# One visit of a chunked recurrence behind each output unit of a fused retention and feed-forward kernel

## The chip, the cores and the metric

One core of one Trainium2 chip. The metric is device time in microseconds (us). Most executions of one kernel agree within about 1 us.

## The reference, cut to what matters

A retention layer (a linear recurrence with a decay per head), then a feed-forward with a leaky ReLU, all in float32:

```python
batch, n_heads, seq, head_dim = (4, 8, 768, 64)
for t in range(S):
    state = gamma * state + einsum('bhd,bhe->bhde', k[:, :, t], v[:, :, t])
    y[:, :, t] = scale * einsum('bhd,bhde->bhe', q[:, :, t], state)
x = y.transpose(0, 2, 1, 3).reshape(3072, 512)
h = x @ w_in                       # 512 -> 2048
return maximum(0.01 * h, h) @ w_out   # 2048 -> 512
```

## The kernel before

The sequence is cut into six parts of 128 tokens, all four batches in each; parts are numbered 0 to 5. For a part and a batch the recurrence is four groups of small matmuls: *scores* (keys against queries, tiles of 64x64), which VectorE masks; *reads* of the running state (64x64); *values* (masked scores against values, 128x64); and *state sums* (128x64). VectorE then *takes* the tokens into x and brings the state up to date. When a part is complete it makes three *differences* t of x.

The feed-forward multiplies in a scheme of seven products instead of eight, M1 to M7, in *hidden units* and *output units* (`seven`). The products share four banks, A to D, of PSUM, the memory that TensorE's products are written to: M1 and then M2 on top of it in A, M6 and M7 in B, M5 and M3 in C, M4 in D. M1 is needed alone, so ScalarE copies it out before M2 is added.

Before the change each part is computed while the part ahead of it is in the feed-forward. TensorE stops twice per two batches: once for their scores, three products later for reads, values and state sums, in banks of their own (two pairs, tag "att").

```python
    def two_banks(name):
        return psum.tile([128, 2, HP, C], FP32, tag="att", bufs=2, name=name)
    def score(c, b):
        x = heads[c, b][0]
        ps = scores[c, b] = two_banks(f"ap_{c}_{b}")
        for a in range(HP):
            for u in range(2):
                for j in range(2):
                    nc.tensor.matmul(ps[ts(u, 64), j, a, :], lhsT=x[ts(j, 64), 1, a, ts(u, 64)],
                                     rhs=x[ts(j, 64), 0, a, :])
    def masked(c, b):
        am = work.tile([128, 2, HP, C], FP32, tag="am", bufs=2, name=f"am_{c}_{b}")
        nc.vector.tensor_tensor(
            out=am.rearrange("p j a t -> p (j a) t"),
            in0=scores[c, b].rearrange("p j a t -> p (j a) t"),
            in1=mask.unsqueeze(1).to_broadcast([128, H, C]), op=ALU.mult)
        scores[c, b] = am
    ...
    def reads(c, b):
        x = heads[c, b][0]
        ps = sums_at[c, b] = two_banks(f"yp_{c}_{b}")
        for j, m, i, a in pairs:
            nc.tensor.matmul(ps[ts(i, 64), j, m, :], lhsT=st[b][ts(j, 64), a, :],
                             rhs=x[ts(j, 64), 0, a, :], start=(m == 0), stop=False,
                             skip_group_check=True)
    def values(c, b):
        if c == 0:
            sums_at[c, b] = two_banks(f"yp_{c}_{b}")
        y, am, ps = heads[c, b][1], scores.pop((c, b)), sums_at[c, b]
        for j, m, i, a in pairs:
            nc.tensor.matmul(ps[ts(i, 64), j, m, :], lhsT=y[:, 1, 2 * a + j, :],
                             rhs=am[:, j, a, :], start=(c == 0 and m == 0), stop=True,
                             skip_group_check=True)
    def state(c, b):
        y = heads.pop((c, b))[1]
        sp = for_state(sums_at[c, b])
        for a in range(HP) if c < NC - 1 else ():
            sums_of(sp, y, a)
    ...
    def tokens_taken(c, b, xb):
        ps = sums_at[c, b]
        th, o = divmod(b * C, N)
        blocks = xb.rearrange("p (kh th) k n -> p kh th k n", th=2)[:, :, th, :, ds(o, C)]
        nc.vector.tensor_tensor(out=blocks, in0=ps[:, :, 0 : HP // 2, :], in1=gq, op=ALU.mult)
    def state_taken(c, b):
        ps = sums_at.pop((c, b))
        if 0 < c < NC - 1:
            nc.vector.tensor_tensor(out=st[b], in0=st[b], in1=for_state(ps), op=ALU.add)
            nc.vector.tensor_tensor(out=st[b], in0=st[b],
                                    in1=gc.unsqueeze(2).to_broadcast([128, HP, D]), op=ALU.mult)
    def products(c, bs):
        for f in (reads, values, state):
            for b in bs:
                f(c, b)
    def stage_y(c, bs, xb):
        products(c, bs)
        for b in bs:
            taken(c, b, xb)
            n = c * B + b + AHEAD
            if c > 1 and n < NC * B:
                load(*divmod(n, B))
    ...
    def differences(x, t, last=True):
        minus(t[:, 0], x[:, 1], x[:, 0])
        minus(t[:, 1], x[:, 3], t[:, 0])
        minus(t[:, 2], x[:, 2], t[:, 1])
        if last:
            last_difference(x)
    ...
    def seven(tiles, name, takes, takes_half=None, order=ORDER):
        banks = {}
        which = [("M1", "A", 0, 0), ("M6", "B", 5, 5), ("M5", "C", 4, 4), ("M4", "D", 3, 6),
                 ("M2", "A", 2, 2), ("M7", "B", 1, 1), ("M3", "C", 6, 3)]
        for m, bank, sa, sb in (which[i] for i in order):
            first = bank not in banks
            split = takes_half is not None and bank == "C"
            if first and split:
                banks[bank] = [two_banks(f"{bank}{i}_{name}")[:, 0].rearrange("p a t -> p (a t)")[:, 0:N]
                               for i in range(2)]
            elif first:
                banks[bank] = psum.tile([128, 2, N], FP32, tag="ff", bufs=4, name=f"{bank}_{name}")
            ps = banks[bank]
            for i in range(2):
                half = ps[i] if split else ps[:, i, :]
                for n, (w, x, t) in enumerate(tiles):
                    rhs = x[:, sb] if sb < 4 else t[:, sb - 4]
                    for k in range(2):
                        nc.tensor.matmul(
                            half, lhsT=block(w, sa)[:, k, ts(i, 128)], rhs=rhs[:, k, :],
                            start=(first and (i == 0 or split) and n == 0 and k == 0),
                            stop=(n == len(tiles) - 1 and k == 1), skip_group_check=True)
                if split and m == "M3":
                    takes_half(i, half)
            if not (split and m == "M3"):
                takes(m, ps)
            yield
    ...
    def hidden(c, u, x, t, g, gd, order=ORDER):
        got = {}
        at = f"{c}_{u}"
        def leaky(i):
            nc.scalar.activation(g[:, i], g[:, i], AF.Prelu, alpha=0.01)
        def takes(m, ps):
            if m == "M1":
                got["m1"] = temp("m1", at)
                nc.scalar.copy(out=got["m1"], in_=ps)
            elif m == "M6":
                got["u2"] = temp("u2", at)
                plus(got["u2"], got["m1"], ps)
            elif m == "M5":
                got["m5"] = temp("m5", at)
                nc.scalar.copy(out=got["m5"], in_=ps)
            elif m == "M4":
                got["m4"] = ps
            elif m == "M2":
                nc.scalar.activation(g[:, 0], ps, AF.Prelu, alpha=0.01)
            elif m == "M7":
                u3 = got["m1"]
                plus(u3, u3, ps)
                plus(g[:, 3], u3, got["m5"])
                leaky(3)
                plus(g[:, 2], u3, got["m4"])
                leaky(2)
            elif m == "M3":
                plus(g[:, 1], got["u2"], ps)
                leaky(1)
                differences(g, gd)
        return seven([(2 * u, x, t)], f"h{at}", takes, order=order)
    ...
    for c in range(2, NC):
        more = c + 1 < NC
        os[c] = new_o(c)
        if more:
            xs[c + 1] = new_x(c + 1)
        for p in range(NU // 2):
            pair = []
            for u in (2 * p, 2 * p + 1):
                pair.append(new_g(c, u))
                at = {}
                if more and u == 2 * p:
                    at = {1: [scored(c + 1, u), scored(c + 1, u + 1)],
                          4: [read(c + 1, u, u + 1)]}
                run(hidden(c, u, *xs[c], *pair[-1][1:]), at)
            at = {1: [differ(c + 1)]} if p == 1 and more else {}
            run(output(c, os[c], pair, p == 0, p == NU // 2 - 1), at)
```

## Time and profile before

| | before |
|---|---|
| median of the first 3 runs, and of all 6 beside the changed kernel | 666.92 us, 666.81 us |
| span of the profiled run | 664.9 us |
| TensorE busy, VectorE, ScalarE | 99%, 56%, 26% |
| TensorE waiting for another engine | 2.2 us, all in the first 13 us |
| stops for the recurrence, parts 2 to 5 | 16 |

The page and the views are read in the prediction below. A row of a timeline reads: start in us, length from the first start to the last end, engine, line, operation, output<-input, shapes, count, and in brackets the idle time before it with what ended it. The lengths of neighbours overlap (in the prediction's lines, 403.20 + 1.89 is past the next start, 404.93), so the difference of two *starts* is what a stretch takes. The first figure of a matmul's shapes, 64\*64, 128\*64 or 128\*128, is the part of TensorE's array that it uses; I call it the *mode*, and 128\*128 *full size*.

I use one further number throughout. The start of an execution varies, so I take from the single records (every matmul's own start in the trace) the time from the start of the first product of the first output unit (58.1 us in) to the end of the last matmul, and call it the **long stretch**. Before: 603.61 us.

### The profile page before, as it was taken

What the parts mean: (1) busy time and instruction counts of PE and PEld (TensorE: products, weight loads), DVE (VectorE), ACT (ScalarE), POOL (GpSimd) and SP (SyncE); (2) the same over time, 40 slices, a digit from 0 to 9 for tenths busy, and PEclk for the clock granted to TensorE, in tenths of its full rate; (3) what the DMA queues carried; (4) which work ended last, traced back from release to release, by engine and by line L of the source; (5) the groups of instructions that cost most, each with busy time, mean ns of one, the idle gap of its engine ahead of it and who ended that gap; (6) DMA issues with size and microseconds to landing.
All of it is one profiled execution on the core that took longest, in us unless ns stands there. A gap on an engine that the chain in (4) does not pass through costs nothing.

```text
span 664.9 us, 10405 instructions
## 1 busy us (share of the span) xinstructions
PE 659.4 (99%) x4505; PEld 573.6 (86%) x4505; DVE 373.9 (56%) x570; ACT 175.8 (26%) x322; POOL 20.1 (3%) x22
## 2 busy tenths in 40 slices
PE   8999999999999999999999999999999999999998
PEld 5888888888888888888888888888888888888886
DVE  5789969889888676325543613663431444431342
ACT  5854555264261002212201311210221220221210
POOL 0000000000000111001000100100100000000000
PEclk9999999999999999999999999999999999999999
DMA  8920312313222453003012100301300001000001
GB/s 327 403 97 33 126 64 79 112 65 113 109 85 75 166 184 127 1 1 128 1 46 81 64 1 1 127 1 64 128 1 0 2 0 45 19 1 1 0 1 63
DMA packets 15758, 48.92 MB, mean 74 GB/s; under 512 B 1753, under 2 KB 2009, under 8 KB 15713
## 3 DMA queue, kind: packets, MB, share of 16 engines
q1 hardware_dynamic: 15696, 48.24, 20.1%
q8 instruction: 35, 0.57, 0.3%
q14 instruction: 11, 0.08, 0.0%
q10 hardware_dynamic: 16, 0.02, 0.0%
HBM read 41.97 MB, written 6.29 MB: 73 GB/s over the span
## 4 chain that ended last, share of the span: by engine, by line
PE 99%; DMA 1%; DVE 0%; issue 0%
PE B_o L414 13%; PE A_o L414 13%; PE C_o L414 12%; PE C_h L414 12%; PE B_h L414 12%; PE A_h L414 12%; PE D_o L414 6%; PE D_h L414 6%; PE ap L165 4%; PE yp L193 4%; PE d L436 2%; PE yp L184 2%; PE yp L208 1%; DMA qk<-in_qk_dram 1%; PE sums L208 0%; PE idle L626 0%
## 5 line engine op out<-in xcount | busy, mean ns | idle before, releaser
L414 PE MATMUL A_h<-x,w 128*128 128x256 f32 x368 | 87.0, 379 | 0.0
L414 PEld LDWEIGHTS A_h<-x,w 128*128 128x128 f32 x368 | 69.9, 190 | 9.6 <-issue 0.2
L414 PE MATMUL A_o<-g,w 128*128 128x256 f32 x288 | 68.0, 379 | 0.0
L449 ACT ACTIVATE g<-g 128x512 f32<-128x512 f32 x69 | 42.0, 630 | 92.4 <-DVE g L361 92.4
L414 PEld LDWEIGHTS A_o<-g,w 128*128 128x128 f32 x288 | 54.8, 190 | 7.4
L454 ACT COPY m<-A_h 128x512 f32<-128x512 f32 x23 | 13.4, 582 | 143.6 <-PE A_h L414 103.9
L361 DVE TENSOR_TENSOR m<-m,B_h 128x512 f32<-128x512 f32 x23 | 15.8, 686 | 55.5 <-PE B_h L414 55.5
L361 DVE TENSOR_TENSOR m<-m,B_o 128x512 f32<-128x512 f32 x16 | 11.0, 685 | 63.9 <-PE B_o L414 63.9
L238 DVE TENSOR_TENSOR x<-yp,dec 128x512 f32<-128x512 f32 x24 | 16.4, 689 | 49.7 <-PE yp L208 35.6
L414 PE MATMUL C_h<-t,w 128*128 128x256 f32 x184 | 44.1, 383 | 0.0
L414 PE MATMUL B_h<-x,w 128*128 128x256 f32 x184 | 44.1, 383 | 0.0
L414 PE MATMUL B_h<-t,w 128*128 128x256 f32 x184 | 43.5, 379 | 0.0
L414 PE MATMUL D_h<-t,w 128*128 128x256 f32 x184 | 43.5, 379 | 0.0
L414 PE MATMUL C_h<-x,w 128*128 128x256 f32 x184 | 43.5, 379 | 0.0
L414 PEld LDWEIGHTS C_h<-t,w 128*128 128x128 f32 x184 | 34.5, 190 | 5.5 <-issue 0.9
L414 PEld LDWEIGHTS B_h<-t,w 128*128 128x128 f32 x184 | 35.0, 190 | 4.7
L414 PEld LDWEIGHTS D_h<-t,w 128*128 128x128 f32 x184 | 35.0, 190 | 4.7
L414 PEld LDWEIGHTS C_h<-x,w 128*128 128x128 f32 x184 | 35.0, 190 | 4.7
L414 PEld LDWEIGHTS B_h<-x,w 128*128 128x128 f32 x184 | 34.5, 190 | 5.0 <-issue 0.3
L364 DVE TENSOR_TENSOR gd<-g,gd 128x512 f32<-128x512 f32 x48 | 37.1, 773 | 1.7
L170 DVE TENSOR_TENSOR am<-ap,mask 128x1024 f32<-128x1024 f32 x24 | 28.5, 1220 | 10.8 <-PE ap L165 10.8
L414 PE MATMUL B_o<-gd,w 128*128 128x256 f32 x144 | 34.0, 379 | 0.0
(118 smaller groups left out, 1019.0 us busy)
## 6 DMA issues: line engine op xcount, KB each, us to landing
raw<-in_weights_dram SPq DMA_DIRECT2D x31, 512.0 KB, 4.3
qk<-in_qk_dram SPq DMA_DIRECT2D x19, 512.0 KB, 3.8
kv<-in_kv_dram SPq DMA_DIRECT2D x17, 512.0 KB, 4.4
out_dram<-o SPq DMA_DIRECT2D x23, 256.0 KB, 2.1
in<-in_qk_dram SPq DMA_DIRECT2D x3, 512.0 KB, 8.7
in<-in_kv_dram SPq DMA_DIRECT2D x3, 512.0 KB, 8.5
kv<-in_kv_dram SPq DMA_DIRECT2D x4, 256.0 KB, 7.0
o_in<-in_qk_dram SPq DMA_DIRECT2D x2, 512.0 KB, 8.6
```

The source lines that it names most:

```text
L165: nc.tensor.matmul(ps[ts(u, 64), j, a, :], lhsT=x[ts(j, 64), 1, a, ts(u, 64)], rhs=x[ts(j, 64), 0, a, :])
L170: nc.vector.tensor_tensor(out=am.rearrange("p j a t -> p (j a) t"), in0=scores[c, b].rearrange("p j a t -> p (j a) t"), in1=mask.unsqueeze ...
L184: nc.tensor.matmul(ps[ts(i, 64), j, m, :], lhsT=st[b][ts(j, 64), a, :], rhs=x[ts(j, 64), 0, a, :], start=(m == 0), stop=False, skip_group_ ...
L193: nc.tensor.matmul(ps[ts(i, 64), j, m, :], lhsT=y[:, 1, 2 * a + j, :], rhs=am[:, j, a, :], start=(c == 0 and m == 0), stop=True, skip_grou ...
L208: nc.tensor.matmul(sp[ts(j, 64), a, :], lhsT=y[:, 0, 2 * a + j, :], rhs=y[:, 1, 2 * a + j, :], start=start, stop=True, skip_group_check=True)
L238: nc.vector.tensor_tensor(out=blocks, in0=ps[:, :, 0 : HP // 2, :], in1=gq, op=ALU.mult)
L361: nc.vector.tensor_tensor(out=out, in0=a, in1=b, op=ALU.add)
L364: nc.vector.tensor_tensor(out=out, in0=a, in1=b, op=ALU.subtract)
L414: nc.tensor.matmul(half, lhsT=block(w, sa)[:, k, ts(i, 128)], rhs=rhs[:, k, :], start=(first and (i == 0 or split) and n == 0 and k == 0), ...
L436: nc.tensor.matmul(banks[r][:, i, :], lhsT=block(2 * u, r + 2 * kh)[:, k, ts(i, 128)], rhs=x[:, 2 * kh + th, k, :], start=(step == 0 and i ...
L449: nc.scalar.activation(g[:, i], g[:, i], AF.Prelu, alpha=0.01)
L454: nc.scalar.copy(out=got["m1"], in_=ps)
```

## The change

Its intent: TensorE should leave its full-size products less often. The scores of the *next* two batches are computed within the visit for the sums of the present two, so that one visit behind each output unit takes the place of two stops. The scores go to the feed-forward's PSUM banks, which are idle between two units once the last sum has read its own. The hidden unit that follows a completed part has its products in the order M1, M2, M6, M5, M4, M7, M3 (`FIRST`), so that two products which need nothing new cover the making of t. A third buffer for masked scores, and loads of queries and keys one visit ahead, make room for it.

The diff, cut to its core; left out are buffer names and small helpers:

```diff
+    def new_am(c, b):
+        i = turn[0]
+        turn[0] = (i + 1) % (3 if (c, b) >= (2, 2) else 2)
+        if i < 2:
+            return work.tile([128, 2, HP, C], FP32, tag=f"am{i}", name=f"am_{c}_{b}")
+        place = new_t(1, f"am_{c}_{b}").rearrange("p i k n -> p (i k n)")[:, 0 : 2 * HP * C]
+        return place.rearrange("p (j a t) -> p j a t", j=2, a=HP)
 ...
-    def stage_y(c, bs, xb):
-        products(c, bs)
 ...
+    def ahead(c, b):
 ...
+            if b == 2:
+                room[c] = new_o(0).rearrange("p i k n -> p (i k n)")
 ...
+    def score_apart(c, b):
+        x = heads[c, b][0]
+        ps = scores[c, b] = [psum.tile([128, HP, C], FP32, tag="ff", bufs=4, name=f"ap{j}_{c}_{b}")
+                             for j in range(2)]
+        for a in range(HP):
+            for u in range(2):
+                for j in range(2):
+                    nc.tensor.matmul(ps[j][ts(u, 64), a, :], lhsT=x[ts(j, 64), 1, a, ts(u, 64)],
+                                     rhs=x[ts(j, 64), 0, a, :])
+
+    def masked_apart(c, b):
+        am = new_am(c, b)
+        for j, ps in enumerate(scores[c, b]):
+            nc.vector.tensor_tensor(out=am[:, j], in0=ps,
+                                    in1=mask.unsqueeze(1).to_broadcast([128, HP, C]), op=ALU.mult)
+        scores[c, b] = am
+
+    def visit(c, b, following=None, complete=False):
+        bs, xb = (b, b + 1), xs[c][0]
+        more = [(following[0], following[1] + i) for i in range(2)] if following else [None, None]
+        early, late = more
 ...
+        do(score_apart, early)
+        for i in bs:
+            reads(c, i)
+        do(masked_apart, early)
+        for i in bs:
+            values(c, i)
+        do(score_apart, late)
+        for i in bs:
+            state(c, i)
+        do(masked_apart, late)
+        for i in bs:
+            tokens_taken(c, i, xb)
+        if complete:
+            if xs[c][1] is None:
+                xs[c][1] = new_t(c, f"t_{c}")
+            differences(*xs[c])
+        for i in bs:
+            state_taken(c, i)
+        for i in bs:
+            if c + 1 < NC:
+                ahead(c + 1, i)
+        for at in more:
+            do(load_kv, at)
+        for at in more:
+            do(decay_v, at)
 ...
+    FIRST = (0, 4, 1, 2, 3, 5, 6)
 ...
-                at = {0: [scored(2, 2 * c), scored(2, 2 * c + 1)],
-                      3: [read(2, 2 * c, 2 * c + 1)]}
-                if c == 1:
-                    put(at, s4=[differ(2)])
+                if c == 0:
+                    at = {0: [scored(2, 0), scored(2, 1)], 3: [lambda: visit(2, 0)]}
+                else:
+                    at = {1: [lambda: ahead(2, 2), lambda: ahead(2, 3)],
+                          2: [lambda: load_kv(2, 2), lambda: load_kv(2, 3)],
+                          4: [scored(2, 2), scored(2, 3)]}
 ...
+    if NC > 2:
+        visit(2, 2, (3, 0) if NC > 3 else None, complete=True)
     for c in range(2, NC):
 ...
-                at = {}
-                if more and u == 2 * p:
-                    at = {1: [scored(c + 1, u), scored(c + 1, u + 1)],
-                          4: [read(c + 1, u, u + 1)]}
-                run(hidden(c, u, *xs[c], *pair[-1][1:]), at)
-            at = {1: [differ(c + 1)]} if p == 1 and more else {}
-            run(output(c, os[c], pair, p == 0, p == NU // 2 - 1), at)
+                run(hidden(c, u, *xs[c], *pair[-1][1:], order=ORDER if u else FIRST), {})
+            run(output(c, os[c], pair, p == 0, p == NU // 2 - 1), {})
+
+            if c + 1 < NC and p == 0:
+                xs[c + 1] = new_x(c + 1)
+                visit(c + 1, 0, (c + 1, 2))
+            elif c + 1 < NC and p == NU // 2 - 1:
+                visit(c + 1, 2, (c + 2, 0) if c + 2 < NC else None, complete=True)
```

More of the change, by code (lines that the diff above doesn't have):

```diff
@@ L166, in score, with new_t, new_o @@
                                      rhs=x[ts(j, 64), 0, a, :])
+    turn = [0]
+    def new_am(c, b):
[5 more added lines that the diff above has]
+        return place.rearrange("p (j a t) -> p j a t", j=2, a=HP)
+    def new_t(c, name):
+        return work.tile([128, 3, 2, N], FP32, tag=f"t{int(c == 1)}", name=name)
+    def new_o(c, name="o"):
+        return work.tile([128, 4, 2, N], FP32, tag=f"o{int(c > 0)}", name=f"{name}_{c}")
     def masked(c, b):
-        am = work.tile([128, 2, HP, C], FP32, tag="am", bufs=2, name=f"am_{c}_{b}")
+        am = new_am(c, b)
         nc.vector.tensor_tensor(
@@ L200, in state @@
     def state(c, b):
-        y = heads.pop((c, b))[1]
+        y = heads[c, b][1]
         sp = for_state(sums_at[c, b])
@@ L251, in products @@
                 f(c, b)
-    def stage_y(c, bs, xb):
-        products(c, bs)
-        for b in bs:
-            taken(c, b, xb)
-            n = c * B + b + AHEAD
-            if c > 1 and n < NC * B:
-                load(*divmod(n, B))
+    def ahead(c, b):
+        if c >= NC:
+            return
+        if b < 2:
+            x = work.tile([128, 2, HP, C], FP32, tag="qk", bufs=AHEAD, name=f"qk_{c}_{b}")
+        else:
+            if b == 2:
+                room[c] = new_o(0).rearrange("p i k n -> p (i k n)")
+            x = room[c][:, ds((b - 2) * 2 * HP * C, 2 * HP * C)]
+            x = x.rearrange("p (s a t) -> p s a t", s=2, a=HP)
+        heads[c, b] = [x, None]
+        load_qk(c, b)
@@ new lines, in load_kv @@
+    def load_kv(c, b):
+        y = work.tile([128, 2, H, D], FP32, tag="kv", bufs=AHEAD, name=f"kv_{c}_{b}")
+        heads[c, b][1] = y
+        nc.sync.dma_start(out=y, in_=kv[c, b])
+    room = {}
+    def score_apart(c, b):
[7 more added lines that the diff above has]
+                                     rhs=x[ts(j, 64), 0, a, :])
@@ new lines, in masked_apart, with do @@
+    def masked_apart(c, b):
+        am = new_am(c, b)
+        for j, ps in enumerate(scores[c, b]):
[6 more added lines that the diff above has]
+        early, late = more
+        def do(f, at):
+            if at is not None:
+                f(*at)
+        do(score_apart, early)
[23 more added lines that the diff above has]
+            do(decay_v, at)
@@ L540, in new_x @@
         x = tile_x(c)
-        t = work.tile([128, 3, 2, N], FP32, tag="t", bufs=2, name=f"t_{c}")
-        return x, t
-    def new_o(c):
-        return work.tile([128, 4, 2, N], FP32, tag="o", bufs=2, name=f"o_{c}")
+        return [x, new_t(c, f"t_{c}") if c < 3 else None]
     slot = [0]
@@ L567, in scored @@
         return do
-    def read(c, *bs):
-        return lambda: stage_y(c, bs, xs[c][0])
     def differ(c):
@@ L585 @@
     place_for(0, 1)
-    place_for(0, 2, new_o("in2"))
-    place_for(0, 3, new_o("in3"))
+    place_for(0, 2, new_o(0, "in"))
+    place_for(0, 3, new_o(1, "in"))
     words = tile_x("words").rearrange("p i k n -> p (i k n)")[:, 0 : 2 * W]
@@ L724 @@
     scored_later(3)
-    later = hidden(1, 0, x1, t1, *parts[1][1:], order=(0, 4, 1, 2, 3, 5, 6))
+    later = hidden(1, 0, x1, t1, *parts[1][1:], order=FIRST)
     next(later)
@@ L755 @@
                     xs[2] = new_x(2)
-                at = {0: [scored(2, 2 * c), scored(2, 2 * c + 1)],
-                      3: [read(2, 2 * c, 2 * c + 1)]}
-                if c == 1:
-                    put(at, s4=[differ(2)])
+                if c == 0:
+                    at = {0: [scored(2, 0), scored(2, 1)], 3: [lambda: visit(2, 0)]}
+                else:
+                    at = {1: [lambda: ahead(2, 2), lambda: ahead(2, 3)],
+                          2: [lambda: load_kv(2, 2), lambda: load_kv(2, 3)],
+                          4: [scored(2, 2), scored(2, 3)]}
             run(output(c, os[c], [parts[c]], u == 0, u == NU - 1), at)
+    if NC > 2:
+        visit(2, 2, (3, 0) if NC > 3 else None, complete=True)
     for c in range(2, NC):
-        more = c + 1 < NC
         os[c] = new_o(c)
-        if more:
-            xs[c + 1] = new_x(c + 1)
         for p in range(NU // 2):
```

## The prediction

> **What bounds the kernel now.** I read the page first, for which engine limits; then the waits of TensorE, for whether it ever stands still; then its timeline around one stop for the recurrence, for what such a stop costs beyond its arithmetic.
>
> ```profile
> span 664.9 us, 10405 instructions
> ...
> PE 659.4 (99%) x4505; PEld 573.6 (86%) x4505; DVE 373.9 (56%) x570; ACT 175.8 (26%) x322; POOL 20.1 (3%) x22
> ...
> PE 99%; DMA 1%; DVE 0%; issue 0%
> ```
>
> TensorE is busy for 99% of the span and is 99% of the chain that ended last; VectorE has 44% to spare, ScalarE 74%. The row of granted clock is 9 in all 40 slices. So only TensorE's records and the gaps between them count. Its waits:
>
> ```profile
> PE idle L626 <- DVE t L621: 1.4, 1, 1.4
> PE ap L165 <- DVE x L238: 0.8, 1, 0.8
> ```
>
> Both are in the first 13 us. After that TensorE waits for nobody. What the change can win is what is lost inside "busy"; what it can lose is any wait it makes. The inside shows in TensorE's timeline of one pair of stops (start, duration, engine, line):
>
> ```profile
> 403.20 1.89 PE L414 MATMUL A_h<-x,w 128*128 128x256 f32 x8
> 404.93 1.89 PE L414 MATMUL B_h<-t,w 128*128 128x256 f32 x8
> 406.75 1.98 PE L165 MATMUL ap<-qk 64*64 64x128 f32 x64
> 408.66 1.99 PE L414 MATMUL C_h<-t,w 128*128 128x256 f32 x8
> 410.49 1.89 PE L414 MATMUL D_h<-t,w 128*128 128x256 f32 x8
> 412.21 1.89 PE L414 MATMUL A_h<-x,w 128*128 128x256 f32 x8
> 414.03 1.10 PE L184 MATMUL yp<-qk,states 64*64 64x128 f32 x32
> 415.07 1.97 PE L193 MATMUL yp<-am,kv 128*64 128x128 f32 x32
> 416.87 1.10 PE L208 MATMUL yp<-kv 128*64 128x64 f32 x32
> 417.90 1.99 PE L414 MATMUL B_h<-x,w 128*128 128x256 f32 x8
> 419.73 1.89 PE L414 MATMUL C_h<-x,w 128*128 128x256 f32 x8
> ```
>
> Read the differences of starts. A product of the feed-forward takes 1.73 (403.20 to 404.93), but the one just before a stop 1.82 and the one just after it 1.83. The stop has two more such losses at its edges. In the single records, steady scores start in groups of four every 109 ns, so 64 of them are 16 x 0.109 = 1.75, where 406.75 to 408.66 is 1.91. From the single records, the loss per stretch against its steady pace is: scores 0.160; the reads of the state (L184) 0.160; L193 with L208 behind it, one stretch in one mode, 0.146 (0.150 where L208 is absent, in the last part); the full-size stretch 0.199 between the stops and 0.204 after the second, both its ends counted. One pair of stops loses 0.160+0.199+0.160+0.146+0.204 = 0.869 us.
>
> **What the Trainium skill says.** "TensorEngine Tiling (Array Packing)", Tiling Modes, Key Properties: changing the tiling mode, not just the tile, drains TensorE. This trace agrees and prices it: every change between 128*128, 64*64 and 128*64 costs 0.15 to 0.20, and L193 to L208, which stays in 128*64, costs none. "TensorE: Matmul & The Clock Gate", Part 2, step 1: only weight loads are pulled ahead, matmuls stay in program order. So a matmul that must wait holds everything behind it; the two waits above agree as far as they go. The same page, Part 1: about 3.4 us of idleness is needed before the clock drops. The waits I expect are under 1 us, so I leave the clock at full; no run here tests it.
>
> **The change part by part.** The start, and parts 0 and 1, keep their order on every engine (I compared the built orders; only names of buffers differ). From part 2 on:
>
> *Mode changes.* Before: 8 pairs of stops (parts 2 to 5, two each), 6 with state sums and 2 without: 6 x 0.869 + 2 x 0.873 = 6.96 us. After: a full visit is scores+reads (64*64, no change between them), values (128*64), scores (64*64), state sums (128*64), then 128*128. That is five changes, as many as the pair of stops had! It saves one full-size return but adds a change from 128*64 to 64*64. Part 1 of the kernel before shows what that one costs:
>
> ```profile
> 32.43 1.09 PE L193 MATMUL yp<-am,in 128*64 128x128 f32 x16
> 33.45 0.67 PE L184 MATMUL yp<-in,states 64*64 64x128 f32 x16
> 34.05 1.09 PE L193 MATMUL yp<-am,in 128*64 128x128 f32 x16
> ```
>
> 32.43 to 33.45 is 1.02 where 8 groups of 0.109 are 0.87: 0.15 for a 128*64 stretch between two others, no less than elsewhere. A full visit loses 0.160+0.150+0.160+0.146+0.204 = 0.82, against 0.869. There are 5 of them (second of part 2, both of parts 3 and 4) = 4.10. The rest: two score stops for part 2 at 0.36 = 0.72; its first visit without scores 0.51; first visit of part 5, without state sums, 0.67; last visit 0.51. Sum 6.51. **Won: 0.45 us**, not the 2 to 3 us that 16 stops made 10 would suggest. The arithmetic itself is the same.
>
> *A new wait.* After the second visit of parts 2, 3, 4 and 5 comes the first hidden unit of the same part, which needs x and t just finished. Its products are reordered: M1, M2, then the ones that need t. That is right for the data (M1 and M2 read x[0] and x[2], which only the first two batches write). But M1 and M2 share bank A, and M2 accumulates onto M1, which ScalarE must first copy out. The built order agrees: the first M2 matmul waits for that copy. In the kernel before M6 stands between them, with a bank of its own. The copy after the M1 of 403.20:
>
> ```profile
> 405.13 0.58 ACT L454 COPY m<-A_h 128x512 f32<-128x512 f32 x1 [8.05 <-PE A_h L414]
> ```
>
> It ends at 405.71; the next product starts at 404.93. With 0.06 for the signal to come back (VectorE's end to TensorE's start at the 0.8 us wait above, by the single records), M2 would start at 405.77: 0.84 late, plus up to 0.10 because its weights cannot be loaded ahead (as C_h after a stop, 1.83 for 1.73). I take 0.9. All of it is on the path, as TensorE has no other work. **Lost: 4 x 0.9 = 3.6 us.**
>
> *Does t come in time?* For the visit at part 3's end, from its start at 0: second scores start at 3.8 and end near 5.0; VectorE masks two halves (half of 1.22 each, about 0.65) to 6.3, takes two batches (0.69 each) to 7.7, then t0 to 8.4, t1 to 9.1, t2 to 9.9. TensorE leaves the visit at 5.9, M1 to 7.8, the wait to 8.7, M2 to 10.4, and only then M6 wants t1. It is 1.3 us early. So the reordering pays one 0.9 wait to avoid one of some 1.4. The first visits are followed by a unit of the older part, which needs nothing new.
>
> *Banks and loads.* The scores sit in feed-forward banks. The built waits are on readers of the preceding product, finished near 0.9, and the second scores want them at 3.8. Loads now come a visit (48 us) ahead, except in part 2: q and k of batches 2 and 3 go into part 0's output buffer, after its stores. The last store should land about 3.2 us into part 1's output (2.1 to land), the loads (3.8 alone, some 2.6 more for the second) at 7.1 and 9.7; the scores want them at 8.6 and 9.6. Tight, perhaps 0.1. I count nothing.
>
> Sum: 666.92 - 0.45 + 3.6 = 670.1 us.
>
> **The rivals.** (a) *Fewer stops, nothing lost*: if a return to full size is the dear part and inner changes are nearly free, six stops fewer bring about 2 us: 665. The lines of part 1 speak against it. (b) *The wait is hidden*, so only 0.45 is won: 666.5. For it, author's care in choosing the order; against it, one bank and a copy that cannot begin before M1 ends. (c) *VectorE becomes the bound at the four boundaries*: late masks and differences delay M6 by another 1 us each: 674. It has 1.3 us in hand. (d) *The loads of part 2 land late*: 1 to 2 us once: 671 to 672. VectorE's and ScalarE's totals hardly change (twelve masks of 1.22 each become pairs of halves, about 0.1 each more), so neither bounds the whole.
>
> **Range and chances.** The switching term is measured to about 0.1 us, the wait to 0.1 each, so 0.4; runs spread 1 us (666.7 to 667.69); (d) adds upward, (b) downward. I say 670.1, range 668.5 to 671.6. 2% is 13 us, which no rival reaches: faster 0.01, same 0.97, slower 0.02.
>
> **What would show it.** TensorE's waits should have a new row, A_h on ScalarE's copy, four times, some 0.7 each, and nothing else over 0.5 after the start. The timeline of a full visit should be 5.9 us long. Score stops should have gone but for two. If M6's B_h waits for VectorE, the chain for t was longer than I made it; if the first scores of batches 2 or 3 of part 2 wait on a DMA, (d) holds. I am wrong as a whole if the time is below 667, that is, if M2 does not wait.

## The result, and the profile after

The changed kernel takes 670.50 us median of 6 runs (670.0 to 673.58), where the kernel before has 666.81: 1.0064 times, 95% interval 1.0044 to 1.0083. That is the same within 2%, and slower beyond noise. The long stretch grows from 603.61 to 606.95 us: 3.34 more.

The page's busy row and chain after:

```profile
PE 661.1 (99%) x4503; PEld 573.7 (86%) x4505; DVE 369.3 (55%) x582; ACT 176.2 (26%) x322; POOL 18.9 (3%) x22
...
PE 98%; DMA 1%; DVE 0%; ACT 0%; issue 0%; SPq 0%; DVEq 0%
```

TensorE does the same work and still bounds the kernel, but ScalarE has appeared in the chain (at 0% as the page rounds it). The waits of TensorE after (total, times, longest) say where:

```profile
PE A_h L500 <- ACT m L540: 2.7, 4, 0.7
PE idle L705 <- DVE t L700: 1.4, 1, 1.4
...
PE d L522 <- DVE w L442: 0.4, 1, 0.4
```

The first row is new: four times 0.68 us of idleness, before the M2 of the first hidden unit of parts 2 to 5. The others are at the start. TensorE's timeline of one visit, the second of part 3, with what surrounds it:

```profile
347.30 1.10 PE L300 MATMUL ap<-qk 64*64 64x128 f32 x32
348.22 1.05 PE L201 MATMUL yp<-o,states 64*64 64x128 f32 x32
349.20 1.97 PE L210 MATMUL yp<-am,kv 128*64 128x128 f32 x32
351.10 1.10 PE L300 MATMUL ap<-qk 64*64 64x128 f32 x32
352.14 1.15 PE L225 MATMUL yp<-kv 128*64 128x64 f32 x32
353.22 1.99 PE L500 MATMUL A_h<-x,w 128*128 128x256 f32 x8
355.89 1.99 PE L500 MATMUL A_h<-x,w 128*128 128x256 f32 x8 [0.68 <-ACT m L540]
357.72 1.89 PE L500 MATMUL B_h<-t,w 128*128 128x256 f32 x8
```

The visit is 5.92 us long, 347.30 to 353.22. The first A_h is M1, the second M2, and B_h is M6. From 353.22 to 355.89 are 2.67 us, where a product takes 1.73. And VectorE and ScalarE in the same stretch:

```profile
353.46 1.28 DVE L255 TENSOR_TENSOR x<-yp,dec 128x512 f32<-128x512 f32 x2
354.77 0.69 DVE L449 TENSOR_TENSOR t<-x 128x512 f32<-128x512 f32 x1
355.25 0.59 ACT L540 COPY m<-A_h 128x512 f32<-128x512 f32 x1 [27.98 <-PE A_h L500]
355.50 1.42 DVE L449 TENSOR_TENSOR t<-x,t 128x512 f32<-128x512 f32 x2
```

ScalarE's copy of M1 ends at 355.84, and M2 starts at 355.89. t1, the first of the last two differences, is made by about 356.2 (half of that row), while M6, which wants it, starts at 357.72.

In the single records every stretch's loss against its steady pace (a full-size matmul every 216 ns, a group of four scores every 109) can be summed. A full visit loses 0.160 (scores and reads) + 0.151 (values) + 0.160 (scores) + 0.147 (state sums) + 0.205 (full size) = 0.823, where the pair of stops lost 0.869. The full-size stretch that holds the wait loses 1.149 instead of 0.205. So each wait costs 0.944: the idle 0.68, and 0.26 at its two ends, where neighbouring matmuls do not overlap as elsewhere.

### The profile page after: what moved, and what is told of

Same layout as the page of the kernel before. It is cut to its first block, busy times and chain, and to the rows that moved or that the text cites. A ratio compares the mean times of both kernels' runs of the same rounds, so it can differ in the third digit from the quotient of the medians.

```text
span 669.9 us, 10441 instructions
## 1 busy us (share of the span) xinstructions
PE 661.1 (99%) x4503; PEld 573.7 (86%) x4505; DVE 369.3 (55%) x582; ACT 176.2 (26%) x322; POOL 18.9 (3%) x22
## 4 chain that ended last, share of the span: by engine, by line
PE 98%; DMA 1%; DVE 0%; ACT 0%; issue 0%; SPq 0%; DVEq 0%
PE B_o L500 12%; PE A_o L500 12%; PE C_o L500 12%; PE A_h L500 12%; PE B_h L500 12%; PE C_h L500 12%; PE D_o L500 6%; PE D_h L500 6%; PE yp L210 4%; PE d L522 2%; PE ap L300 2%; PE ap L165 2%; PE yp L201 1%; PE yp L225 1%; DMA qk<-in_qk_dram 1%; ACT m L540 0%
## 5 line engine op out<-in xcount | busy, mean ns | idle before, releaser
L449 DVE TENSOR_TENSOR gd<-g,gd 128x512 f32<-128x512 f32 x48 | 33.2, 692 | 1.7
L500 PE MATMUL D_o<-gd,w 128*128 128x256 f32 x144 | 34.0, 379 | 0.0
L500 PE MATMUL C_o<-g,w 128*128 128x256 f32 x144 | 34.0, 379 | 0.0
```

Of the source, the lines that this page charges most:

```text
L449: nc.vector.tensor_tensor(out=out, in0=a, in1=b, op=ALU.subtract)
L500: nc.tensor.matmul(half, lhsT=block(w, sa)[:, k, ts(i, 128)], rhs=rhs[:, k, :], start=(first and (i == 0 or split) and n == 0 and k == 0), ...
```

## The experiments

My theory after the result: four waits of M2 for ScalarE's copy lose 4 x 0.944 = 3.78 us, and the visits themselves win 0.45. Its rivals: the visits are dear and the wait would only move elsewhere if removed; the reordering is needless; mode changes inside a visit are nearly free, so that the sum is right by accident. All kernels gave correct results. "Against before" is the ratio with its 95% interval; the last column is the difference of long stretches.

| run | median, before beside it | against before | long stretch | less that of before |
|---|---|---|---|---|
| changed kernel | 670.50, 666.81 | 1.0064 (1.0044 to 1.0083) | 606.95 | +3.34 |
| c1_after_again | 670.45, 666.99 | 1.0054 (1.0039 to 1.0070) | 606.95 | +3.34 |
| e1_own_bank | 666.76, 667.65 | 0.9993 (0.9974 to 1.0012) | 603.18 | -0.43 |
| e2_plain_order | 671.99, 667.65 | 1.0064 (1.0048 to 1.0080) | 607.92 | +4.31 |
| e3_scores_together | 668.80, 667.65 | 1.0024 (1.0005 to 1.0044) | 605.40 | +1.79 |
| e4_before_reordered | 674.01, 667.65 | 1.0088 (1.0071 to 1.0104) | 608.74 | +5.13 |
| e5_both | 665.17, 666.99 | 0.9979 (0.9963 to 0.9996) | 601.63 | -1.98 |
| e6_copy_twice | 673.03, 666.99 | 1.0102 (1.0083 to 1.0121) | 609.42 | +5.81 |
| e7_other_buffer | 671.36, 666.94 | 1.0065 (1.0044 to 1.0086) | 607.38 | +3.77 |
| e8_scores_around | 665.06, 666.94 | 0.9980 (0.9959 to 1.0002) | 601.46 | -2.15 |

**The changed kernel again.** 

> The changed kernel again, unaltered, as the measure for the two beside it: 3.3 us above the kernel before by the theory (0.45 won, 3.8 lost), 670.2.

It came to 670.45 us and the same long stretch as the first profile, to 0.01 us. Its whole span is 671.6 where the first had 669.9: the start differs, the rest does not.

**M2 in its own bank.** 

> The changed kernel with M2 of the first hidden unit of parts 2 to 5 in a bank of its own: VectorE adds M1's copy to it and ScalarE takes the leaky part, so M2 no longer waits for the copy. Theory (the whole loss is M2 waiting for ScalarE's copy, 0.945 us four times, and mode changes win 0.45): the four waits are gone, M6 still comes after t is ready (in the changed kernel t1 is ready 1.5 us before M6 starts, so 0.6 are left), and the time is 0.45 us below the kernel before, about 666.4. Rival (TensorE would wait for t instead, the wait only moves): about 669 or more, with B_h waiting for VectorE. Rival (the visits themselves cost the time): stays at 670.

```diff
+            bank = "E" if m == "M2" and apart else bank
 ...
+            elif m == "M2" and apart:
+                plus(g[:, 0], got["m1"], ps)
+                leaky(0)
 ...
-                run(hidden(c, u, ..., order=ORDER if u else FIRST), {})
+                run(hidden(c, u, ..., order=ORDER if u else FIRST, apart=u == 0), {})
```

TensorE's waits in this kernel:

```profile
PE idle L709 <- DVE t L704: 1.4, 1, 1.4
PE ap L165 <- DMA in<-in_qk_dram: 1.0, 1, 1.0
PE ap L165 <- DMA qk<-in_qk_dram: 0.2, 1, 0.2
```

Nothing is left after the start: the four waits are gone and no wait for t has taken their place, though M6 now comes 0.94 earlier. The long stretch falls by 3.77 us against the changed kernel (3.78 expected) and is 0.43 below the kernel before (0.45 expected). By the clock of whole runs it is 0.9993 times before, not to be told from it. This refutes the rival that the wait only moves.

**The copy made longer.** 

> The changed kernel with ScalarE's copy of M1 made twice in those four units (the same result): the suspected wait is lengthened and nothing else. Theory: each wait grows by one copy, about 0.6 us, 4 x 0.6 = 2.4: 672.6 to 672.9, waits of about 1.3 us. Rival (the copy is not what the time hangs on): no change, 670.2.

```diff
                 nc.scalar.copy(out=got["m1"], in_=ps)
+                if c > 1 and u == 0:
+                    nc.scalar.copy(out=got["m1"], in_=ps)
```

```profile
PE A_h L500 <- ACT m L542: 5.2, 4, 1.3
```

The dose shows in the response: waits of 1.3 us, and 2.47 us more on the long stretch than the changed kernel for four added copies (2.4 expected). Together with the run before it, this shows the copy to be on the path, at its full length.

**The old order after a visit.** 

> The changed kernel with the old order of products (M1, M6, ...) in those four units, so that M1 and M2 are apart again. Theory: M6 then stands for t1, which is ready 1.2 us after M6 could start (0.9 in part 5), plus 0.1 for weights that cannot be loaded ahead: 3 x 1.3 + 1.0 = 4.9 lost in place of 3.8, time about 671.3, with four waits of B_h on VectorE near 1.0 us each. Rival (the reordering is what costs, and t would be in time without it): 666.4.

```diff
-                run(hidden(c, u, ..., order=ORDER if u else FIRST), {})
+                run(hidden(c, u, ..., order=ORDER), {})
```

```profile
PE B_h L500 <- DVE t L449: 3.8, 4, 1.1
```

Now M6 stands for t, up to 1.13 us. The single records put the loss at 1.37 each in parts 2 to 4 (1.57 lost instead of 0.205) and at 0.65 in part 5: 4.74 in all against e1_own_bank, where the reordered products lose 3.77. It is 0.97 slower than the changed kernel, on the long stretch, so the reordering was worth having; it bought a cheaper wait with a dearer one. I had 4.9 for this sum; part 5's was over-sized.

**The reordering alone, in the kernel before.** 

> The kernel before, with the new order of products (M1, M2, M6, ...) in the first hidden unit of parts 2 to 5, and nothing else changed: stops, loads and banks as before. Theory (M2 after M1 in one bank must wait for the copy, whatever surrounds it): four waits of 0.68 us and 4 x 0.945 = 3.8 lost: 670.6. Rival (the wait comes of the visits, with ScalarE or VectorE behind): no wait here, 666.8.

```diff
-                run(hidden(c, u, *xs[c], *pair[-1][1:]), at)
+                run(hidden(c, u, *xs[c], *pair[-1][1:],
+                           order=ORDER if u else (0, 4, 1, 2, 3, 5, 6)), at)
```

This one missed: 5.13 us, not 3.8. The waits are four all right, but one is of 2.0 us (part 2), and there ScalarE's copy itself had to wait, as its timeline shows:

```profile
244.14 0.59 ACT L454 COPY m<-A_h 128x512 f32<-128x512 f32 x1 [19.02 <-DVE o L361]
```

M1 itself had ended at 242.74 (240.85 and 1.89). The copy's buffer, m1, was still read by VectorE's sums of the last output unit, and VectorE was late with them, having made part 2's differences in between. In parts 3 to 5 the loss is 0.94 as expected. By whole runs this kernel is 6.4 slower, not 5.1. The starts (below) account for that as far as the record goes: five of its six runs have a mean granted clock of 0.997; the sixth, at 1.000, took 672.14, which is 5.2 above 666.91, the median of the runs of the kernel before at 1.000 beside it, its one slow start left out. So M2 behind M1 in one bank waits without any visit; how long depends on the copy's own buffer too.

**The same with another buffer for the copy.** 

> e4_before_reordered (the kernel before with the new order of products alone) lost 5.1 us in its trace, not 3.8: three waits of 0.68, but that of part 2 was 2.04, its copy itself standing for VectorE until 244.1. Theory: there the copy waits for its buffer (m1), which the last output unit's sums still read, late because VectorE also makes part 2's differences then. Here M1's copy in those four units goes into the buffer of u2, free since early in the output unit, and u2 into that of m1. Expected: four waits of 0.68 us, 1.36 less than e4, 3.8 above the kernel before: 670.6 to 671. Rival (ScalarE or the clock is behind in part 2, not the buffer): the wait stays at 2.04 and the time at that of e4.

```diff
-                got["m1"] = temp("m1", at)
+                got["m1"] = temp("u2" if c > 1 and u == 0 else "m1", at)
 ...
-                got["u2"] = temp("u2", at)
+                got["u2"] = temp("m1" if c > 1 and u == 0 else "u2", at)
```

```profile
PE A_h L414 <- ACT u L454: 2.7, 4, 0.7
```

Four equal waits, and 3.77 us lost against 3.8 expected. The miss of the run before it is settled.

**Both batches' scores at the head of a visit.** 

> The changed kernel with both batches' scores at the head of the visit, so a visit has three mode changes in place of five; its waits at M2 stay. Theory (each change drains and costs 0.15 to 0.2 whatever lies between): a full visit loses 0.51 in place of 0.82, five of them win 0.31 each and that of part 5 0.155: 1.7 us below the changed kernel, about 668.5 to 668.7. Rival (a change inside a visit is nearly free, only the return to full size costs): no difference, 670.3. Rival (the second scores stand for their banks, freed 0.9 us into the visit): a wait of ap for VectorE and less won.

```diff
         do(score_apart, early)
+        do(score_apart, late)
         for i in bs:
             reads(c, i)
 ...
-        do(score_apart, late)
         for i in bs:
             state(c, i)
```

The lines of `values` between the two places are left out. It wins 1.55 us on the long stretch against the changed kernel, where 1.71 were expected: a visit loses 0.51 in place of 0.82, as the price of a change says, so changes inside a visit are not nearly free. The missing 0.16 is one wait of the kind that the last rival named, in part 2 alone. TensorE's timeline there:

```profile
236.64 2.04 PE L300 MATMUL ap<-qk 64*64 64x128 f32 x61
238.44 0.27 PE L201 MATMUL yp<-o,states 64*64 64x128 f32 x1
238.50 0.28 PE L300 MATMUL ap<-qk 64*64 64x128 f32 x3
```

This head of a visit loses 0.327 instead of 0.160. The second scores' last bank is read by the output unit's last sum, which ran on VectorE from 236.95 to 237.63, behind three other sums that had started at 235.02, as soon as the product before was done. The scores wanted the bank 0.92 after 236.64, at 237.56, and went on at 237.67.

**Both repairs.** 

> Both repairs in one: M2 in a bank of its own and both batches' scores at the head of a visit. Theory: no wait at M2, 0.45 + 1.7 of mode changes saved against the kernel before: 664.6, faster than both kernels by 0.3% or more. Rival (with the wait gone and the visit shorter, M6 comes before t): up to 1 us lost again at each of four places, with B_h waiting for VectorE: 665 to 668.

The edits are those of e1_own_bank and e3_scores_together. The second visit of part 3, in TensorE's timeline:

```profile
344.05 1.98 PE L300 MATMUL ap<-qk 64*64 64x128 f32 x64
345.85 1.05 PE L201 MATMUL yp<-o,states 64*64 64x128 f32 x32
346.83 1.97 PE L210 MATMUL yp<-am,kv 128*64 128x128 f32 x32
348.63 1.10 PE L225 MATMUL yp<-kv 128*64 128x64 f32 x32
349.66 1.99 PE L501 MATMUL A_h<-x,w 128*128 128x256 f32 x8
351.49 1.89 PE L501 MATMUL E_h<-x,w 128*128 128x256 f32 x8
353.22 1.03 PE L501 MATMUL B_h<-t,w 128*128 128x256 f32 x4
```

The visit is 5.61 us, and M2 (E_h) and M6 (B_h) follow at once. 665.17 us is 0.9979 times the kernel before, interval 0.9963 to 0.9996: it is below both kernels, by little (the same within 2%). The long stretch is 1.98 below before; 2.15 were expected, and the difference is the 0.17 of part 2's bank again.

**The second scores behind the reads.** 

> e5_both, with the second batch's scores moved behind the reads of the state, in the same tiling mode, so that a visit still has three mode changes. In e5 and e3 the scores at the head of part 2's second visit stood 0.167 us for a bank that VectorE freed 1 us into the visit. Theory: this wait goes, the other visits stay at 0.51 lost: 0.17 us less than e5, 664.4 to 665.0, and 601.46 us from the first output product to the last matmul, where e5's trace has 601.63. Rival (going from scores to reads and back costs): 0.3 us or more above e5.

```diff
         do(score_apart, early)
         for i in bs:
             reads(c, i)
+        do(score_apart, late)
 ...
-        do(score_apart, late)
```

The diff is against the changed kernel; M2's own bank, as in e1_own_bank, is left out of it. The second visit of part 3:

```profile
344.30 1.10 PE L300 MATMUL ap<-qk 64*64 64x128 f32 x32
345.22 1.05 PE L201 MATMUL yp<-o,states 64*64 64x128 f32 x32
346.10 1.05 PE L300 MATMUL ap<-qk 64*64 64x128 f32 x32
347.08 1.97 PE L210 MATMUL yp<-am,kv 128*64 128x128 f32 x32
```

From 344.30 to 347.08 are 2.78 us, exactly as in e5_both (344.05 to 346.83), where the reads come last.

The second scores and the reads change places within one tiling mode, and part 2's wait is gone (that head loses 0.160 now): the long stretch is 601.46 us, 0.17 less than e5_both, to the hundredth what was expected. Whole runs cannot tell these two apart (665.06 and 665.17); against the kernel before its interval reaches 1.0002, as two of its six runs had the slow start. No change of product inside one mode shows a cost.

## Why the prediction was right

- *TensorE alone bounds.* Right: every difference between the kernels is a loss of TensorE that its own records show, and they add up to 0.03 us.
- *Mode changes: 0.45 won.* Right: e1_own_bank, the change without the wait, wins 0.43. The parts were right too (0.823 for a visit; 0.82 was said). The intent failed here: a visit has as many mode changes as the two stops that it replaces.
- *The wait at M2: 0.9, four times.* The mechanism was right (e1, e6, e4 and e7 show it from four sides), the size a little low: 0.944 each. I had 0.84 from the end of the copy and left most of the loss for weights not loaded ahead (up to 0.10) as a rounding; all of it is lost.
- *t comes in time, and the reordering buys one wait with another.* Right: t1 was 1.5 us early (1.3 was said), and e2_plain_order is dearer by 0.97.
- *Banks and loads add nothing.* Right for the changed kernel. The tight loads of part 2 were issued at 227.0, 4.8 us before the scores that need them, and nothing waited; rival (d) is out. The bank that VectorE frees late did cost 0.17, but only after e3 moved the second scores to the front.
- *The clock stays full through the waits.* Right where it mattered: after the waits of 0.68, and after that of 2.04 in e4_before_reordered, the matmuls follow each other by 216 ns again from the second one on. At the start it was not so (see below).
- *Sum.* 3.15 us was predicted, 3.34 measured on the long stretch; the median came to 670.5 where 670.1 was said, in the range. The rest of the runs' difference lies outside the long stretch, and starts differ between executions: three of the changed kernel's twelve timed runs are over 671.9 and the other nine within 669.7 to 670.6.

The traces show what differs at the start. Groups of small matmuls start every 213 ns instead of 109 until 5.8 us in the profile of the kernel before, but until 13.7 us in c1_after_again (673.40 us) and just so in e7_other_buffer (673.82 us), which has no visits; so slow starts do not come of the change. In the changed kernel's first profile (671.96 us) the granted clock was 1.00 from 5.2 to 8.5 us, 0.50 from 8.6 to 11.9, and 1.00 after. What remains open is why the full clock comes late, or goes once more, in some executions; no run here tests it.

## What to carry to other kernels

Count mode changes of TensorE, not stops: putting the small matmuls into one visit won 0.43 us in all here, and making the groups of one mode adjacent, as in e8_scores_around, 0.31 more per visit. When products are reordered to cover a wait for data, look at which PSUM banks become neighbours: accumulating onto a bank that another engine must first copy out costs that copy and both ends of the gap (0.944 us for a copy of 0.59). An engine with half its time free can still hold up a bank or a buffer, if its queue puts other work in front (VectorE, 56% busy, made the copy late in e4_before_reordered: a wait of 2.0 us).

## What the Trainium skill lacked or had wrong

- "TensorEngine Tiling (Array Packing)", Tiling Modes, says that a change of mode drains TensorE, but gives no price. Here a stretch in one mode between two others loses 0.146 to 0.161 us if its tiles are small, and 0.197 to 0.205 if it is full-size; a change of the kind of product within a mode costs nothing that shows.
- "TensorE: Matmul & The Clock Gate", Part 3, puts the starts of matmuls on different tiles about 4 ns apart. Here four matmuls on 64x64 tiles start 5 to 8 ns apart (float32), and the next four 109 ns after the first four.
- The same page, Part 1, calls the slow clock at the start run-variable, but puts it at about 3.4 us, and lets it come back after an idle window of about 3.4 us. Here the slow pace lasted until 13.7 us in c1_after_again, 12.3 us after the first matmul, with TensorE busy for 12.25 of them. In the changed kernel's first profile the clock fell to 0.50 at 8.6 us, although TensorE's only wait in the 3.3 us before was one of 0.73. The granted clock that the view gives for c1_after_again's start is 1.00; it does not show the slow pace, which the starts of the matmuls do.
- No page that I read prices an accumulation onto a bank just copied by another engine: TensorE idle for 0.68 us around a copy of 0.59, 0.944 lost.
